# A fused cross attention and SwiGLU block: first weights made in the output weights' space, stores and spills as streams, six step orders re-dealt

## The chip, the cores and the metric

One core of one Trainium2 chip. The metric is the device time of one execution in microseconds; of several runs the median is taken. The engines have these names: PE is TensorE, PEld its weight loads, DVE VectorE, ACT ScalarE, POOL GpSimd, SP SyncE.

## The reference

```python
B, H, S, Ns, D = (8, 8, 512, 32, 64)
a = softmax(x @ state.T / sqrt(D));   xread = a @ state      # 512 tokens read 32 states
a2 = softmax(state @ x.T / sqrt(D));  sread = a2 @ x         # 32 states read 512 tokens
x = concatenate([xread, sread], axis=2)                      # heads side by side: (8 * 544, 512)
xn = x / sqrt(mean(x * x) + 1e-06) * rms_g
g = xn @ w_gate                                              # 512 x 1536
out = (silu(g) * (xn @ w_val)) @ w_out                       # 1536 x 512
```

So for each of 8 batches 512 token rows and 32 state rows are read by attention, scaled by RMS, and sent through three weight matrices. x and the states come as float32; the three weight matrices arrive in 64-bit form and are converted by the kernel itself.

## The kernel before

**The work of a batch.** For each batch the kernel loads the states (L137) and x (L142, L147, L155) and computes scores of all heads at once. For batches 2 and later x is transposed on DVE (L357, from `x_b` to `xB`), stored to memory as `x_d` from ACT's queue (L359), loaded back as `xG` by four DMAs from ACT's queue (L364), and multiplied with the states on PE (L374). The token read follows (L430 the exponential on ACT, L456 on PE, squares for the RMS at L463 on ACT, scaled rows `aT_s` at L469 on DVE). The state read goes the same way: exponentials on ACT (L629), a transpose on DVE (L647, `eB`), a store to `e_d` (L650) and four loads (L654) on ACT's queue, then the products with x on PE (L665). Since the rows of a token read are mixtures of only 32 states per head, gate and value weights are first multiplied with the states ("own weights": `own_weights`, PE L730, copied out by ACT at L742 as `v`, combined further by POOL).

**The feed-forward.** The 1536 columns are 12 blocks, taken as 6 pairs. Batch 0 goes plainly (`hidden`: PE L773, silu on ACT L779, product on DVE L783), its hidden rows `hb` are spilled to memory as `h_d` (L785) and projected at the very end. Batches 1 to 7 and the state rows use products in the manner of Strassen: `hidden_seven` makes seven products where eight would stand (PE L882; copies out on ACT L929, L932, L934; silu on ACT L936; sums on DVE L945, L958). The projection is `project_seven` for batch 1 and the states, `project_twice` (two levels, PE L1170, ACT L1183, POOL L1198, DVE L1210 to L1229) for the others. Its weights are sums of quarters of the output weights, kept in memory as `t_d`.

**The weights.** The raw weights arrive as 18 pieces of 1 MB, gate and value of each pair in turn and then six output pieces; four raw buffers let four pieces be under way, and the load of piece k+4 (L240) is issued when piece k has been converted (ACT L273 and L276, DVE L297 and L301). The tile `wo` (12 blocks of 512 columns) takes the output weights. Gate weights and value weights of a pair share one tile of 1 MB. In the kernel before, it lies in the pool `ws` of three buffers (`new_w`, name `w_m`), and when its value part is converted, SP stores it to memory as `w_d` (L305). From then on every batch fetches its six pairs from `w_d` into the three `ws` buffers again (L222), pair n+3 when pair n has been used.

**The order of the work.** Nothing is scheduled automatically on PE, DVE, ACT, POOL and SP: each stage is a generator ("stream") that issues a few instructions per step, and strings of letters say which stream takes the next step. ORDER covers batch 0 (letters that include the preparation), batch 1 (lower case) and batch 2 (upper case), PERIOD is used for each of batches 3 to 6, LAST for batch 7 and STATES for the state rows together with batch 0's projection. An engine works through its instructions strictly in the order issued, and a DMA is issued by the engine in whose program it stands: a waiting instruction holds up all behind it on that engine.

Of the kernel before, what the change touches and what calls it, by code (L numbers as in the profile page):

```python
# [21 lines left out]
W_BUFS = 3  # L22
# [1 line left out]
ZERO = 16 * 896  # L24

ORDER = (
    "zzzz11z11113111zzzz18883133121228221119991998825515222z1662262666116622665555511"
    "9226122880226666644200955555889988i446666655i99ji000iijmm888i5i6995998990jj66i80"
    "0iimm896988966669j000ijimii86899j8mm899000i68ii8906i9666666666jm800jm88i6998i6ij"
    "j7796767imm7ni877777jnnnn8nnnnihht799798mtv89ht7788hhuuthuuhh9thu9txhhhtuuxxfff8"  # L30
    "8hu99qqvqtvhahxtthhhtxuuhxhuuuhxaaxhtutthaahtfhxvxxqaaqfuhhuutuuhthhthtLaauhuhuu"
    "uthhutxhtaaqhhthhhquualuuuutuhuuaaaaaaaaqqaaaaaaaaaaauppppaqppaakkccckdaqquapaaa"
    "dkaaaaapaccawcwxxxssssspwxVssddsskpkkkppkkpdddddddddddddxfsXkxkssspsssddddddddHH"
    "dccddTHTHTHUXXUVVHHTTHTUHHTUUHHHHHUUUHTXTHTTlAXAAAXAHHHAHHUUUUTTXXUTAHHUUXFTVXXX"
    "HHHHHeUUUTUHTHUUUTHHKTHHGAHKKAUAAeUUTUHeKTHTHHUUUTUUHUTUUAAAAAHUUKAPPPPCPPKKFPKK"
    "KKPPPPKKKKCAPPPPKKPPPPAAAAAAAPPPCGPPKKKPPKPKPPCCCFFAAAAAAGGAAAKKKKKKAFSAPPPPPSSP"
    "SSAKAAPPPPAAAAASSSSSPPKPKOOPSSKOAOPAWWWXXXXXKGLPGKPKKKKOOXPSSCPPGFSSCOO"
)

PERIOD = (  # L40
    "vahhthtxthahhhhxuutxuthahaaathatuuhluhhuhtvtvfxutuxhaxhthaghuaxhhxuauutfuxhhukkk"
    "tthhhthgauvuhtuhhkthtauhaaxaxtauhhuausufufxhutsththhaugauuthuhuughupaptuhsuuupkg"
    "kpkkpkkapppkcppkkpkppcgpppkkpkaapopkspaaapkpkkpppasacpkaaccksppkpkkpcaakspkpaaak"
    "asaappskpksspskppkaakppkgoooppppkaakappppkasoalwfswossxpxfxcwxxxcoo"
)

LAST = (
    "fvhthhtthxxhuuthuxvvuhththuhhhthhuuthattxxxuahhhuutuhuhvhxxxtuththhhauuhtuuhkkff"
    "fhatxhuukhtthxxhuguhthhuuuutuuhhtahthhthuuuutuuupphupkkkpkkkupppkppkkkpppccppppp"
    "pppkkkkkkkkkkkkkkkkkaappppppppgcppppcpcggkpppaackkkkpppakkoooopppppppcpppkcoooo"  # L50
)
STATES = (
    "hthththhhyyyyyuutuuhththuhthrrrhhuutyrhthtyuhyyyhhtrhhuuuuuyhyytytrhthhthhhhhuuu"
    "uuhyyyyyytththhthhhuuuuuuuKKKthuuuuKKththhtuhuuKKtuPPughuKKKKPPPPPPPbguCgPPKPgKK"
    "KgKggPPKKCPPPPbPPPPKKKbKKKKKKKPPPPPPCCPPPPPKPKCPPPPOOCKbbKKKPKPPbKKKKKKOPKOOPPPP"
    "CPPPbCOppkpkkccppkkOOkcpkkpkpc"
)


# [1 line left out]
def kernel(  # L61
# [20 lines left out]
    nc = tc.nc  # L82
    VE, SE, GE, TE = nc.vector, nc.scalar, nc.gpsimd, nc.tensor

    B, H, S, D = x.shape
# [4 lines left out]
    NI = DM // P  # L90
    NM = DFF // P
# [102 lines left out]
    w_d = [scratch.tile([P, NI, 2, 2, P], F32, name="w_d%d" % mp) for mp in range(NM // 2)]  # L194
# [17 lines left out]
    raw = {}  # L212

    def new_w(n):

        w_sb[n] = ws.tile([P, NI, 2, 2, P], F32, name="w_m")
        return w_sb[n]

    def fetch(n):

        if NM // 2 <= n < (B + 1) * (NM // 2):
            nc.sync.dma_start(out=new_w(n), in_=w_d[n % (NM // 2)])  # L222
# [57 lines left out]
    def values():  # L280
        for k in range(len(pieces)):
            for a in parts(k):
                if a.start == 0:
                    to = home(k)
                    if k in raw:
                        words = raw[k].rearrange("p f four -> p (f four)").bitcast(U32)
                        words = words[:, 0:16 * P].rearrange("p (f two) -> p f two", two=2)[:, :, 1]
                dst = to[:, a]
                if k not in raw:
                    src = pieces[k].rearrange("p a (c f) -> p a c f", f=P)  # L290
                    for i in range(a.start, a.stop):
                        nc.sync.dma_start(out=to[:, i], in_=src[:, i])
                    yield
                else:
                    c = columns(k, a)
                    word, rest = words[:, c], words[:, c].bitcast(I32)
                    VE.tensor_scalar(rest, word, 2.0 ** -13, 2.0 ** 19 - 1, op0=ALU.mult, op1=ALU.min)  # L297
# [3 lines left out]
                    VE.tensor_tensor(out=dst.bitcast(I32), in0=rest, in1=top, op=ALU.bitwise_or)  # L301
                if a.stop == pieces[k].shape[1]:
                    mp, kind = places[k]
                    if kind == 1:
                        nc.sync.dma_start(out=w_d[mp], in_=w_sb[mp])  # L305
                    raw.pop(k, None)
                    load_piece(k + RAW_AHEAD)
                yield
# [453 lines left out]
    def hidden(m, lhs, rhs):  # L762


        gp, vp = [], []
        t = []
        h = hb[:, m, :]

        def products():
            for k, to in enumerate((gp, vp)):  # L770
                to.append((fx.tile([P, S], F32, name="f") if m % 2 else vps.tile([P, S], F32, name="pv")))
                for i, r in enumerate(rhs):
                    TE.matmul(out=to[0], lhsT=lhs(i, k), rhs=r,  # L773
                              start=(i == 0), stop=(i == len(rhs) - 1))
# [12 lines left out]

        return products(), silu(), gated()
# [583 lines left out]
    def first_batches():  # L1372
# [75 lines left out]
```

## Time and profile before

| | |
|---|---|
| median of 3 runs | 760.8 us (759.03 to 761.41) |
| profiled execution | 761.82 us |
| its span | 759.8 us |
| mean granted PE clock | 0.993 |
| PE busy | 739.1 us, 97% |
| DVE busy | 576.9 us, 76% |
| ACT busy | 355.4 us, 47% |
| POOL busy | 265.3 us, 35% |
| moved by DMA | 152.46 MB, mean 201 GB/s |

How to read it: the span runs from the first to the last recorded instruction, and some 2 us of the execution's time lie around it. The shares are means over very different stages: batch 0 with the conversion of the weights (to about 88 us), batch 1 (to about 137), batch 2 (to about 260), then periods of 80 us each for batches 3 to 7, and the state rows with batch 0's projection at the end.

### The profile page before, as it was taken

To read this page: it belongs to the slowest core of one execution; us is meant where nothing else is said; L and a number is where in the kernel's file an instruction comes from. 1 tells how busy PE (TensorE), PEld (TensorE's weight loads), DVE (VectorE), ACT (ScalarE), POOL (GpSimd) and SP (SyncE) were. 2 spreads that over 40 slices of the span, in tenths; PEclk is the share of its full clock that TensorE was granted. 3 is DMA by queue.
4 is the path that set the end of the run, shared out by engine and by line. 5 is a ranking of instruction groups with operands and counts; after the bars stand their busy time and mean duration, and the time that the engine had idled before them with its cause. 6 is when DMAs were issued, how large, how long until landed. Compare 5 with 4: busy or idle time off the path is not lost.

```text
span 759.8 us, 14397 instructions
## 1 busy us (share of the span) xinstructions
PE 739.1 (97%) x5660; PEld 605.3 (80%) x5660; DVE 576.9 (76%) x963; ACT 355.4 (47%) x616; POOL 265.3 (35%) x360
## 2 busy tenths in 40 slices
PE   8998989999999799999999999999999999999998
PEld 7532567777888677997799878987898689999997
DVE  5886678979699747994799469955998368977952
ACT  5987974433543255626472547335642552122110
POOL 1400534043402644129312851266223761330451
PEclk9999999999999999999999999999999999999999
DMA  8999896048636582378518870877166722256421
GB/s 233 361 364 418 298 408 195 6 141 300 265 79 268 167 319 56 134 266 276 159 56 300 261 217 1 302 238 261 29 256 201 268 105 63 77 209 228 126 63 53
DMA packets 60667, 152.46 MB, mean 201 GB/s; under 512 B 10420, under 2 KB 30392, under 8 KB 53688
## 3 DMA queue, kind: packets, MB, share of 16 engines
q1 hardware_dynamic: 49552, 132.59, 49.1%
q10 hardware_dynamic: 11048, 18.95, 8.7%
q8 instruction: 45, 0.74, 0.4%
q14 instruction: 22, 0.18, 0.1%
HBM read 119.61 MB, written 31.92 MB: 199 GB/s over the span
## 4 chain that ended last, share of the span: by engine, by line
PE 72%; DVE 11%; DMA 9%; ACT 4%; issue 3%; POOL 1%; SPq 0%; ACTq 0%; DVEq 0%; POOLq 0%
PE f L882 30%; PE f L1170 26%; PE f L1026 5%; DMA w_m<-w_d 4%; PE pv L730 3%; DMA x_d<-xB 2%; DMA raw<-in_moe_w_val_dram 2%; PE at L730 1%; PE pv L773 1%; DVE w L1124 1%; PE at L374 1%; PE f L1318 1%; ACT ex L276 1%; DVE hb L958 1%; ACT lin L273 1%
## 5 line engine op out<-in xcount | busy, mean ns | idle before, releaser
L882 PE MATMUL f<-aT_s,v 128*128 128x256 f32 x504 | 119.5, 381 | 0.7 <-ACT g L934 0.7
L882 PEld LDWEIGHTS f<-aT_s,v 128*128 128x128 f32 x504 | 94.6, 190 | 22.2 <-DVE h L1224 3.4
L945 DVE TENSOR_TENSOR g<-g,f 128x512 f32<-128x512 f32 x84 | 56.1, 685 | 62.8 <-PE f L882 41.6
L882 PE MATMUL f<-aT_t,vs 128*128 128x256 f32 x336 | 86.8, 382 | 2.0 <-ACT g L929 2.0
L1183 ACT COPY kept<-f 128x512 f32<-128x512 f32 (+1 forms) x56 | 29.9, 536 | 110.0 <-PE f L1170 110.0
L1198 POOL TENSOR_TENSOR kept<-kept 128x256 f32<-128x256 f32 x28 | 21.6, 771 | 167.2 <-DVE kept L1210 114.1
L1170 PE MATMUL f<-w,h 128*128 128x128 f32 x588 | 74.7, 276 | 0.2 <-DVE h L1220 0.2
L882 PEld LDWEIGHTS f<-aT_t,vs 128*128 128x128 f32 x336 | 62.7, 190 | 14.1 <-issue 4.4
L757 POOL TENSOR_TENSOR vs<-v 128x256 f32<-128x256 f32 x42 | 32.1, 764 | 116.7 <-ACT v L742 116.5
L1170 PEld LDWEIGHTS f<-w,h 128*128 128x128 f32 x588 | 69.8, 192 | 0.7 <-DVE h L1220 0.4
L936 ACT ACTIVATE hb<-g 128x1024 f32<-128x1024 f32 x42 | 44.4, 1057 | 49.5 <-DVE g L945 45.0
L318 POOL TENSOR_TENSOR ri<-ss,mhalf 128x4 f32<-128x4 f32 (+1 forms) x9 | 8.5, 948 | 116.7 <-ACT ss L406 103.2
L958 DVE TENSOR_TENSOR hb<-hb,f 128x512 f32<-128x512 f32 x42 | 28.6, 682 | 24.6 <-PE f L882 24.5
L882 PE MATMUL f<-aT_t,v 128*128 128x256 f32 x168 | 43.9, 383 | 0.0
L882 PE MATMUL f<-aT_s,vs 128*128 128x256 f32 x168 | 43.4, 380 | 0.0
L1170 PE MATMUL f<-wo,hb 128*128 128x128 f32 x336 | 42.3, 275 | 0.0
L1170 PE MATMUL f<-wo,h 128*128 128x128 f32 x336 | 42.1, 275 | 0.0
L1170 PEld LDWEIGHTS f<-wo,hb 128*128 128x128 f32 x336 | 40.3, 192 | 1.1 <-issue 0.8
L958 DVE TENSOR_TENSOR hb<-hb,c 128x512 f32<-128x512 f32 x42 | 32.9, 784 | 9.4 <-ACT hb L936 9.2
L1170 PEld LDWEIGHTS f<-wo,h 128*128 128x128 f32 x336 | 39.8, 192 | 0.0
L934 ACT COPY g<-f 128x512 f32<-128x512 f32 x42 | 24.8, 590 | 31.1 <-PE f L882 31.1
L882 PEld LDWEIGHTS f<-aT_t,v 128*128 128x128 f32 x168 | 31.0, 190 | 9.1 <-issue 3.4
(256 smaller groups left out, 1659.5 us busy)
## 6 DMA issues: line engine op xcount, KB each, us to landing
w_m<-w_d SPq DMA_DIRECT2D x48, 1024.0 KB, 7.2
w<-t_d SPq DMA_DIRECT2D x49, 576.0 KB, 6.7
out_dram<-kept SPq DMA_DIRECT2D x32, 256.0 KB, 4.1
raw<-in_moe_w_val_dram SPq DMA_DIRECT2D x6, 1024.0 KB, 9.7
w_d<-w_m SPq DMA_DIRECT2D x6, 1024.0 KB
raw<-in_moe_w_out_dram SPq DMA_DIRECT2D x6, 1024.0 KB, 12.4
x_b<-in_x_dram SPq DMA_DIRECT2D x6, 1024.0 KB
x_d<-xB ACTq DMA_DIRECT2D x6, 1024.0 KB, 5.5
```

Source lines behind the costliest of these rows:

```text
L318: GE.tensor_tensor(out=ri[:, 0:n], in0=ss, in1=mhalf[:, 0:n], op=ALU.pow)
L730: TE.matmul(out=pv[e][Ns * j:Ns * j + Ns, :], lhsT=stT_g[b][D * e:D * e + D, j, :], rhs=w[D * e:D * e + D, j].rearrange("p m k f -> p (m k ...
L757: GE.tensor_tensor(out=vs[:, 0], in0=a21, in1=a22, op=ALU.add)
L882: TE.matmul(out=ps[:, i, 0:half], lhsT=l[:, i, :], rhs=r, start=(start and i == 0 and k == 0), stop=(k == len(lhs) - 1), skip_group_check= ...
L934: SE.copy(gates(q)[1], q["x"][:, :, 0:half])
L936: SE.activation(out=hid(2 * mp, 2 * mp + 2)[:, :, 0:n].rearrange("p m (c t) -> p m c t", c=2), in_=q["g"][:, :, :, 0:half], func=ACTF.Silu ...
L945: VE.tensor_tensor(out=to, in0=to, in1=q[ps][:, :, 0:half], op=ALU.add)
L958: VE.tensor_tensor(out=part, in0=part, in1=val, op=ALU.mult)
L1026: TE.matmul(out=banks[name][:, r, :], lhsT=lhs(k)[:, P * r:P * r + P], rhs=rhs(k), start=(start and r == 0 and k == 0), stop=(k == HM - 1) ...
L1170: TE.matmul(out=to[half][:, slot, :], lhsT=lhs[:, k, :], rhs=rhs[:, k, :], start=(fresh and n in (0, 4) and k == 0), stop=(k == QM - 1), s ...
L1183: SE.copy(of_half(k, i), banks[name][i])
L1198: GE.tensor_tensor(out=k[:, 4:8:3], in0=k[:, 5:6].to_broadcast([P, 2, QD]), in1=k[:, 4:8:3], op=ALU.add)
```

## The change

1. The converted gate and value weights of pairs 0 to 2 are made in the `ws` buffers and stay there for batch 1, which no longer fetches them. Those of pairs 3 to 5 are made in `wo`, into whose space the output weights come later.
2. The six stores to `w_d` and the six spills to `h_d` are no longer issued by the steps that finish the values, but by two streams of their own, "b" and "y", whose place is given by letters.
3. All orders are dealt anew, with the same letters but for the 12 new ones: ORDER has 883 steps instead of 871; the counts of PERIOD, LAST and STATES are the same.

```diff
 def fetch(n):
-        if NM // 2 <= n < (B + 1) * (NM // 2):
+        if NM // 2 + W_BUFS <= n < (B + 1) * (NM // 2):
             nc.sync.dma_start(out=new_w(n), in_=w_d[n % (NM // 2)])
 def home(k):
...
-        return (w_sb[mp] if kind else new_w(mp))[:, :, :, kind, :]
+        if kind == 0:
+            first_w[mp] = (new_w(mp) if mp < W_BUFS else
+                           wo[:, NI * (mp - W_BUFS):NI * (mp - W_BUFS) + NI].rearrange(
+                               "p i (m k f) -> p i m k f", m=2, k=2))
+            w_sb[mp] = first_w[mp]
+            if mp < W_BUFS:
+                w_sb[mp + NM // 2] = first_w[mp]
+        return first_w[mp][:, :, :, kind, :]
 def values():
...
-                    mp, kind = places[k]
-                    if kind == 1:
-                        nc.sync.dma_start(out=w_d[mp], in_=w_sb[mp])
                     raw.pop(k, None)
                     load_piece(k + RAW_AHEAD)
 def gated():
             VE.tensor_tensor(out=h, in0=t[0], in1=vp[0], op=ALU.mult)
-            if m % 2:
-                nc.sync.dma_start(out=h_d[m // 2], in_=hb[:, m - 1:m + 1])
             yield
+    def weights_kept():
+        for mp in range(NM // 2):
+            nc.sync.dma_start(out=w_d[mp], in_=first_w[mp])
+            yield
+    def gated_kept():
+        for mp in range(NM // 2):
+            nc.sync.dma_start(out=h_d[mp], in_=hb[:, 2 * mp:2 * mp + 2])
+            yield
...
-                   "z": keep_awake()}
+                   "b": weights_kept(), "y": gated_kept(), "z": keep_awake()}
```

Of the four strings the beginning of PERIOD stands for all:

```diff
-    "vahhthtxthahhhhxuutxuthahaaathatuuhluhhuhtvtvfxutuxhaxhthaghuaxhhxuauutfuxhhukkk"
+    "vhhaththhaaatuhhhaauxxavvutthhtthhhhxuuuuututhhuhxxthtuaahuhhuaaxxtutfghlhukktht"
```

What the new strings do to the programs of the engines is seen in rows of those programs. In the changed kernel the line numbers are 5 to 30 higher. First SP in batch 0 and the beginning of batch 1, before: raw pieces (L240), stores of weights (`w_d`, L305), spills (`h_d`, L785), fetches (L222).

```order
L305 DMA w_d_129<-w_m 128x2048
L240 DMA raw<-in_moe_w_val_dram 128x4x1024
L785 DMA h_d_136<-hb 128x1024
L240 DMA raw<-in_moe_w_gate_dram 128x4x1024
L305 DMA w_d_130<-w_m 128x2048
L240 DMA raw<-in_moe_w_val_dram 128x4x1024
L240 DMA raw<-in_moe_w_gate_dram 128x4x1024
L785 DMA h_d_137<-hb 128x1024
L305 DMA w_d_131<-w_m 128x2048
L240 DMA raw<-in_moe_w_val_dram 128x4x1024
L240 DMA raw<-in_moe_w_out_dram 128x2x2048
L222 DMA w_m<-w_d_128 128x2048
```

The same stretch now (raw pieces L249, stores L1277, spills L1283, fetches L224, x L143):

```order
L1277 DMA w_d_129<-w_m 128x2048
L249 DMA raw<-in_moe_w_val_dram 128x4x1024
L249 DMA raw<-in_moe_w_gate_dram 128x4x1024
L249 DMA raw<-in_moe_w_val_dram 128x4x1024
L249 DMA raw<-in_moe_w_out_dram 128x2x2048
L1277 DMA w_d_130<-w_m 128x2048
L1277 DMA w_d_131<-wo 128x2048
L249 DMA raw<-in_moe_w_out_dram 128x2x2048 x3
L1277 DMA w_d_132<-wo 128x2048
L1277 DMA w_d_133<-wo 128x2048
L249 DMA raw<-in_moe_w_out_dram 128x2x2048 x2
L1283 DMA h_d_136<-hb 128x1024
```

The store of the third pair moved from among the gate and value pieces to behind the first output piece, the spills moved behind the last raw piece, and the first fetch of all is now that of `w_d_131`, after x of batch 2 has been issued.

Second, ACT around the store and the loads of x in batch 3, before (`g`, `hb` and `c` are the seven products' copies and silus, `v` the own weights):

```order
L359 DMA x_d_135<-xB 128x4x512
L934 COPY g<-f 128x2x256
L936 ACTIVATE hb<-g 128x1024
L929 COPY g<-f 128x2x256
L742 COPY v<-at 128x512
L932 COPY c_3156<-f 128x512
L742 COPY v<-at 128x512
L364 DMA xG<-x_d_135 32x4x512
L934 COPY g<-f 128x2x256
L364 DMA xG<-x_d_135 32x4x512 x2
```

And now (store L365, loads L370, the copies L933, L936 and L938, silu L940, own weights L748):

```order
L365 DMA x_d_135<-xB 128x4x512
L940 ACT_TABLE_LOAD
L940 ACTIVATE hb<-g 128x1024
L933 COPY g<-f 128x2x256
L936 COPY c_3111<-f 128x512
L938 COPY g<-f 128x2x256
L940 ACTIVATE hb<-g 128x1024
L933 COPY g<-f 128x2x256
L748 COPY v<-at 128x512 x2
L936 COPY c_3149<-f 128x512
L938 COPY g<-f 128x2x256
L370 DMA xG<-x_d_135 32x4x512 x4
```

Between the store and the first load 6 instructions stood, and now 11 stand, and the four loads go together.

Third, ACT at the turn from batch 2 to batch 3, before (exponentials L629, squares' sums L406, `e_d` stored at L650 and loaded at L654):

```order
L629 ACTIVATE e_2123,z_2126<-sS,s_2124 128x4x128 x2
L406 ACTIVATE ss<-at,bounds 32x4 x4
L650 DMA e_d_143<-eB 128x1024
L654 DMA e_2123<-e_d_143 32x4x256 x4
L742 COPY v<-pv 128x512 x2
```

And now (exponentials L635, `e_d` stored at L656, squares L469, kept parts of the projection L1187, `e_d` loaded at L660):

```order
L635 ACTIVATE e_2039,z_2042<-sS,s_2040 128x4x128
L656 DMA e_d_143<-eB 128x1024
L469 ACTIVATE sq<-pv 128x512
L1187 COPY kept<-f 128x384
L469 ACTIVATE sq<-pv 128x512
L469 ACTIVATE sq<-at 128x512 x2
L660 DMA e_2039<-e_d_143 32x4x256 x4
L412 ACTIVATE ss<-at,bounds 32x4 x4
L687 ACTIVATE sr<-at,z_2042 128x64 x2
L748 COPY v<-pv 128x512 x2
```

The store moved ahead of the squares and of their sums (L412), and five instructions now stand between it and the loads, which followed it directly before.

More of the change, by code (lines that the diff above doesn't have):

```diff
@@ L26 @@
 ORDER = (
[L27 to L37, printed above, removed]
+    "zzzz11z1133411441311zzz88z111111222229995288932665582255z66161816622552621299555"
@@ new lines @@
+    "88225551119900026115b255852226698ii908j6667668800ii99j7iii897mmb96776866666660ji"
+    "jmm00iii98998898866jm6900088ii997bb777jj98i66m000mi96886i998966ijbb666666ji08i80"
+    "46mi06688m99999iy8yy6jj886iijm778m7nnnnnninnnhthh9t8ytm88hhuuthhhttu99h99977vxxx"
+    "uhthhh8hhuuutttuhhth9qqqhvxxxvxxuufuuhhxahltaataatuuaahhhqutuhuhvhttuuhthhhtqqqq"
+    "xxxuaayuuuhuaahhttuhthhhyhthquuuuuuuqtaaaaaahuuuufppcaaacppcaacddaaaqppaaaaaaaak"
+    "kdddadkkaaakppaaaaafdcfcpdaassdsddaddssssssssapkLkkkwwxfwppxxddxkkfqppdddkscsddl"
@@ L38 @@
+    "dsdddddddcVxHHTTHTHHHHUUTTsAxHTAUUHUHHTHVVHXHAsAXXAAAUUUTTUHTHUHTXXXHUXXXHHHUTTH"
+    "TAUHHTAUUKeeAHHUUTAFVXHUUHTHTXXKKHHTKHHHAHHUUUUUUTTTeHHHHTHUAAAGAAAUUUUUUTGPPAAH"
+    "PPUUUCUPPPKKKKKKAAAPPKAPPKKCPPPPPPPPKPPPPKKKSKSFFAFSSKKPPPKKKAAPPCPPAAAAKPCCAPSS"
+    "KSPACAPKKPKKPPAGAASPPPOAAOPSSSAAAKAKAGPLSPPKOAOAPSSWWXXXWXXKKFFPCKPPKPKKOXGOSSCO"
+    "OGG"
 )
 PERIOD = (
-    "vahhthtxthahhhhxuutxuthahaaathatuuhluhhuhtvtvfxutuxhaxhthaghuaxhhxuauutfuxhhukkk"
-    "tthhhthgauvuhtuhhkthtauhaaxaxtauhhuausufufxhutsththhaugauuthuhuughupaptuhsuuupkg"
@@ L43 @@
-    "kpkkpkkapppkcppkkpkppcgpppkkpkaapopkspaaapkpkkpppasacpkaaccksppkpkkpcaakspkpaaak"
-    "asaappskpksspskppkaakppkgoooppppkaakappppkasoalwfswossxpxfxcwxxxcoo"
+    "vhhaththhaaatuhhhaauxxavvutthhtthhhhxuuuuututhhuhxxthtuaahuhhuaaxxtutfghlhukktht"
+    "xhkkuhuhuaavxhhtttaaxauuafxxhfuuhshthhhhuutuuahththhtsuuhuuutppuhaauuupauskkpppp"
+    "pcpkkpppppakpkkkkkgkfckakgaskkaakkppppppppapsappkoocccppcaaakkppasspaaakkapkksss"
+    "sppppppgppkpaakpgkppkooasalffaaapkkppcaakkkkaswwogosssgxxppxcoowxxx"
@@ L51 @@
 )
 STATES = (
[L53 to L56, printed above, removed]
+    "htyhhththhryyhhuuuyhtyuththhtuhhyuutuhhthyyyythhuuthhhuuuyyyyyyrrtththhhuutuuhhr"
+    "urrhhtuuyyuythtthuuyhhhuuhKtttKKKhhtuuuuhuhuthuPKuKPuhuKKKKKKKgPgPPPPPPPPPPPggCP"
+    "gggKPPKKKPCPPKPCCPPPKKKKKKPPKKKKKKKPKPPKPPCCPPPPPKKKKPPKPPPPKKKKPPPPPPOOOOOObbbP"
@@ L57 @@
+    "CbbbbCppkkkuccpppkkkkOcpkppkOc"
 )
@@ L212 @@
     raw = {}
+    first_w = {}
     def new_w(n):
```

6 lines of the change are left out of this document (3 added, 3 removed).

## The prediction

> **What bounds the kernel now.** I read the page's busy shares first, then a table of windows by stage, and then, engine by engine, the rows of the timeline that carry an idle time.
>
> ```profile
> span 759.8 us, 14397 instructions
> PE 739.1 (97%) x5660; PEld 605.3 (80%) x5660; DVE 576.9 (76%) x963; ACT 355.4 (47%) x616; POOL 265.3 (35%) x360
> ```
>
> TensorE (PE) is busy for 739.1 of 759.8 us, and the change issues the same matmuls. So whatever the change gives must come out of 20.7 us of idle PE, a few of them before the first matmul, and out of time in which PE ran at a lower clock. The windows say where both lie. Each row is a stretch in us, its length, busy time and count for PE, PEld, DVE, ACT, POOL, then the granted PE clock, the DMA share and GB/s.
>
> ```profile
> 29.30:64.00 34.70, 34.32 (x208) 12.91 (x207) 27.95 (x44) 30.07 (x37) 5.70 (x10) 1.00 0.99 365
> 64.00:68.00 4.00, 1.61 (x5) 0.40 (x3) 1.22 (x2) 2.96 (x4) 0.00 (x0) 1.00 1.02 429
> 68.00:71.60 3.60, 3.60 (x12) 1.07 (x20) 3.53 (x6) 3.00 (x5) 0.00 (x0) 0.53 1.01 416
> 71.60:88.40 16.80, 16.80 (x91) 7.56 (x92) 11.00 (x16) 14.95 (x25) 3.91 (x5) 1.00 0.80 298
> 88.40:137.00 48.60, 44.76 (x316) 33.62 (x315) 39.58 (x57) 29.06 (x42) 21.79 (x24) 1.00 0.81 289
> 260.00:263.30 3.30, 0.00 (x0) 0.00 (x0) 1.37 (x3) 0.00 (x0) 3.22 (x5) 0.92 0.84 287
> 263.30:270.00 6.70, 6.65 (x94) 4.78 (x95) 0.00 (x0) 1.64 (x5) 6.46 (x10) 0.53 0.84 292
> 430.40:510.40 80.00, 80.00 (x664) 68.41 (x663) 62.92 (x106) 40.15 (x74) 33.34 (x46) 1.00 0.60 199
> ```
>
> The last row is a steady batch: PE is never idle, DVE works 62.92 and ACT 40.15 of 80 us. Nothing can be won there, and something can be lost. The losses stand in four other places: batch 0 (up to 88.4), batch 1 (88.4 to 137), the end of batch 2 (260 to 270), and two later spots shown below.
>
> **Batch 0.** PE rows, then ACT, then the chain of waits:
>
> ```profile
> 67.98 3.61 PE L773 MATMUL pv<-aT_s,v 128*128 128x512 f32 x4 [2.39 <-ACT sq L463]
> 72.54 1.98 PE L773 MATMUL pv<-aT_s,v 128*128 128x512 f32 x4
> ```
> ```profile
> 65.01 1.25 ACT L273 ACTIVATE lin<-raw,bounds 128x1024 f32<-128x1024 int16 x1 [2.82 <-DMA raw<-in_moe_w_val_dram]
> ```
> ```profile
> 29.21 0.61 DVE raw L297
> 30.15 1.18 DVE w_m L301
> 50.15 0.34 SPq L305
> 50.59 14.34 DMA raw<-in_moe_w_val_dram
> ```
>
> PE waited 2.39 us for ACT's L463, which stood in ACT's program behind a conversion waiting 2.82 us for a raw weight piece. That piece took 14.34 us, and just ahead of it on SP, at 50.15, stands a 1 MB store of converted weights. At the 365 to 429 GB/s of these windows, 1 MB costs 2.4 to 2.9 us of the DMA engines, which are full (share 0.99 to 1.02): about the wait. Then the clock fell: the same four matmuls take 3.61 us instead of 1.98, and 3.60 us at 0.53 lose 3.60 x 0.47 = 1.7 us. So the place costs 4.1 us. In the new order the third store comes three pieces later and the spills of h come after the last raw piece, so both parts should go. Against it stands the start: the last write of aT_s on DVE now has a conversion of 1024 columns more ahead of it (0.61 + 1.18 = 1.8 us by the chain rows), so the first L773 comes about 2 us later. What is late next is ACT: its busy time from 29.3 to 88.4 is 30.07 + 2.96 + 3.00 + 14.95 = 51.0 us, and PE's need without the loss is 59.1 - 4.1 = 55.0 us. That is 4 us of slack. I take 4.1 - 2 = **+2.1**; bounds -1.9 (only the late start shows) and +4.1.
>
> [...]
>
> **Batch 1.** It no longer fetches the weights of pairs 0 to 2, since the first copies are kept.
>
> ```profile
> 91.83 1.09 PE L730 MATMUL pv<-w_m,stT_g 64*32 64x512 f32 x16 [0.45 <-DMA w_m<-w_d]
> 106.03 1.09 PE L730 MATMUL pv<-w_m,stT_g 64*32 64x512 f32 x16 [1.64 <-DMA w_m<-w_d]
> 130.71 1.10 PE L882 MATMUL f<-aT_t,vs 128*128 128x256 f32 x4 [1.35 <-ACT g L929]
> ```
> ```profile
> 89.52 16.46 DMA w_m<-w_d
> 119.06 8.76 DMA x_d<-xB
> ```
>
> The first two waits are for fetches, the second for one that took 16.46 us. Both fetches fall away: 0.45 + 1.64 = **+2.1**. Price of the cover: the next three pairs, made in the space of the output weights, are fetched into ws buffers that come free only when pairs 0 to 2 have been used. If that is late, the wait stands at pair 3 instead of pair 1 and nothing is gained: bounds 0 and 2.1. The output pieces must now wait for the stores that read their space. Their cost, from nothing to one conversion (0.61 + 1.18 us of DVE), lies inside batch 0's bounds.
>
> **Gathering x.** The 1.35 us at 130.71 is ACT's: the load of xG stands in ACT's program and waits for the store x_d, 8.76 us under way, and L936 and L929 queue behind it. The same happens once more later:
>
> ```profile
> 119.06 0.41 ACTq L359 DMA_DIRECT2D x_d<-xB  x1
> 127.84 0.82 ACTq L364 DMA_DIRECT2D xG<-x_d  x2
> 129.04 1.06 ACT L936 ACTIVATE hb<-g 128x1024 f32<-128x1024 f32 x1 [4.23 <-DVE wo L1009]
> ```
> ```profile
> 529.14 0.59 ACT L934 COPY g<-f 128x512 f32<-128x512 f32 x1 [2.88 <-PE f L882]
> ```
> ```profile
> 529.78 0.92 PE L882 MATMUL f<-aT_s,v 128*128 128x256 f32 x3 [0.72 <-ACT g L934]
> ```
> ```profile
> 518.92 9.85 DMA x_d<-xB
> ```
>
> Store to load is 8.8 us at the first place and 9.9 us at the second. Before, 4 ACT instructions stood between the two in batch 2 and 6 later; now 8 and 11. These come at PE's pace, so the distance about doubles, and neither wait should remain: 1.35 + 0.72 = **+2.1**, bounds 0 and 2.1. The score matmuls that need xG stay behind 54 matmuls of L882, as before, and three of four loads stand where they stood, behind the same copy. If that cover fails, it is at most the 4.23 us that ACT lost at 129.04.
>
> **The turn from batch 2 to 3.**
>
> ```profile
> 252.61 0.34 ACTq L650 DMA_DIRECT2D e_d<-eB  x1
> 255.31 1.76 ACTq L654 DMA_DIRECT2D e<-e_d  x4
> ```
> ```profile
> 263.35 1.93 PE L665 MATMUL at<-x_b,e 128*32 128x64 f32 x64 [3.39 <-issue]
> ```
>
> PE reaches L665 at 259.96 and waits 3.39 us. Its exponents go through memory: stored at 252.61, loaded from 255.31 on, so 10.7 us from store to first use. At the next steady turn the trace puts no idle time there, and the same matmuls take 1.03 us instead of 1.93. The clock row gives 6.70 us at 0.53, which lose 6.70 x 0.47 = 3.1 us: 6.5 us in all. In the new order the store stands 12 groups of L1170 ahead of L665; before it was 8 groups and two L730. Twelve groups of six at 0.67 us, by the chain of a steady turn,
>
> ```profile
> 425.29 1.03 PE at L665 x64
> 427.60 0.67 PE f L1170 x6
> 430.40 9.71 PE f L882 x44
> ```
>
> are 8.0 us. The trip needs 2.7 us to the store's landing (252.61 to 255.31), 1.76 for four issues, and the landing of the last load, which here ended at 263.35, 6.3 us after 257.07. A weight fetch was under way then, and the new order has none near. With the last part between nothing and 6.3 us the trip is 4.5 to 10.7 us, so the wait that is left lies between 0 and 2.7. I take 1.5 without a fall of the clock: 6.5 - 1.5 = **+5.0**, bounds 0 (a left wait of 2.4 us was enough to lower the clock in batch 0) and 6.5.
>
> **Own weights of pairs 3 and 4.** In each of five batches their products now come after 16 matmuls of L882 instead of 30; their fetches still start when pairs 0 and 1 have been used.
>
> ```profile
> 427.53 0.42 SPq L142 DMA_DIRECT2D x_b<-in_x_dram  x1
> 428.05 1.70 SPq L222 DMA_DIRECT2D w_m<-w_d  x2
> ```
> ```profile
> 598.87 1.21 PE L730 MATMUL pv<-w_m,stT_g 64*32 64x512 f32 x16 [1.14 <-DMA w_m<-w_d]
> ```
> ```profile
> 590.33 8.41 DMA w_m<-w_d
> ```
>
> L665 starts at 425.29 in this batch, the first L882 at 430.40, the two fetches at 428.05. A matmul of the program is two of the page's, so 16 of L882 take 32 x 9.71 / 44 = 7.1 us, and the product of pair 3 comes at about 437.5, 9.5 us after its fetch was issued. By the 8.41 us of the last row that is enough, by the 16.46 us of the fetch in batch 1 it is 7 us too little, once; two fetches go out together, and the product of pair 4 follows at once. I take a value near the first row, a wait of 0.4 us in each of five batches: **-2.0**; bounds 0 and -7.5 (1.5 us each, somewhat over the 1.14 of this place).
>
> **What costs nothing.** ACT_TABLE_LOADs fall from 24 to 16; in steady batches ACT has 40 us to spare (40.15 of 80). The wait of 1.14 us at 598.87 and the stage of the states I leave as they are, with bounds -2 and +1.1. The stores as streams of their own move the same bytes.
>
> [...]
>
> **Sum.** 2.1 + 2.1 + 2.1 + 5.0 - 2.0 = 9.3 us. The profiled execution took 761.82 us, its span 759.8 plus 2.0 around it; 761.8 - 9.3 = 752.5. It lies 1.0 above the median of the three runs, 760.8, so the forecast is **751.5 us**.
>
> **Rivals.** R1, a wait takes another's place: the fetches for pairs 3 and 4 land late in every batch. 1.5 us in five batches is 7.5 instead of 2.0, so 751.5 + 5.5 = 757.0. For it speaks the 1.14 us at 598.87, against it the steady batch without any idle PE.
>
> R2, slower: DVE's program now has two of the four transposes of x_b (L357) ahead of the first sum of the first pair (L945) and two right behind it; before, all four stood behind three such sums.
>
> ```profile
> 434.28 1.38 DVE L945 TENSOR_TENSOR g<-g,f 128x512 f32<-128x512 f32 x2 [7.73 <-PE f L882]
> 436.44 2.48 DVE L357 STREAM_TRANSPOSE xB<-x_b 128x512 f32<-128x512 f32 x4
> ```
>
> If x_b is not there, DVE stops and with it the sums that free PE's accumulators. Before, the transposes began at 436.44, 8.9 us after x_b was issued; the first sum starts at 434.28, 6.8 us after it. The new order issues x_b ahead of an output store, so somewhat sooner, and I put the point from which the mechanism decides at 9 us under way for x_b. At 12 us, between the 8.41 and 16.46 us of the two fetches of 1 MB above, DVE is blocked for 3 us; with 2.5 of it on PE in five batches that is 12.5 us: 751.5 + 12.5 = 764.0. Against it: DVE idles 17 us of a steady batch, and the fetch of 8.41 us is inside the 9.
>
> R3, the change doesn't give what it removes: batch 0 becomes ACT-bound (0 of 2.1) and the turn keeps its wait (0 of 5.0): 751.5 + 7.1 = 758.6, about no change.
>
> **How the numbers follow.** A measurement of this kernel can tell about 0.3%, or 2.3 us, from no change. Forecast (747 to 756) 0.57, R1 0.13, R2 0.18, R3 0.12. Of R3 two thirds fall within 0.3%, of R2 nearly all are slower, and the forecast and R1 are faster but for a small part of each: faster 0.68, same 0.14, slower 0.18. The range takes in the forecast's bounds below (all terms at their best and no loss at the fetches: 761.8 - 2.1 - 4.1 - 2.1 - 6.5 - 1.1 - 1.0 = 744.9, so 745) and reaches up to R2's 764, part of R2 left out above.
>
> **What would show it.** Right: no idle PE and no clock near 0.53 around 68 and 263 us; no fetch in batch 1 before pair 3; the loads of xG issued without ACT idle behind them. R1 would show as L730 released by the fetch about 12 us after each L665; R2 as DVE idle before L357, released by x_b, and PE idle at L882; R3 as PE waiting for ACT in batch 0. I am wrong if the new order makes waits at places where the old one has none, since I priced only the edits I could find in it.

## The result, and the profile after

The changed kernel takes 750.39 us at the median of four runs, the kernel before 760.04 us. The ratio is **0.9866, 95% interval 0.9837 to 0.9896**: 1.3% faster, about 9.7 us, where 751.5 us had been forecast. One run of the four, the profiled one, took 1930.91 us, PE busy for 1922.7 us of it with the same 5660 matmuls (the 504 of L886 from `aT_s` and `v` for 315.1 us instead of 120.2), so the profile read here is that of a second set of runs of the same kernel (750.22 us, ratio 0.9885, interval 0.9856 to 0.9914), whose profiled execution has this span and these busy times:

```profile
span 747.6 us, 14397 instructions
PE 733.0 (98%) x5660; PEld 604.5 (81%) x5660; DVE 576.7 (77%) x963; ACT 344.4 (46%) x608; POOL 262.3 (35%) x360
```

The span is 12.2 us shorter than that of before, more than the 9 to 10 us between the medians: the profiled execution of before was one of the slower ones of its kernel. The windows of the same stages, columns as before the prediction (length, the five engines' busy time, PE clock, DMA share, GB/s):

```profile
64.00:68.00 4.00, 4.00 (x24) 1.63 (x9) 2.97 (x3) 3.97 (x6) 0.00 (x0) 1.00 1.01 428
68.00:71.60 3.60, 3.60 (x23) 1.08 (x22) 3.38 (x7) 3.57 (x6) 0.00 (x0) 1.00 1.00 380
71.60:85.40 13.80, 13.80 (x127) 6.37 (x126) 10.43 (x16) 12.53 (x19) 5.51 (x7) 1.00 1.02 410
85.40:134.00 48.60, 48.60 (x281) 38.04 (x279) 43.32 (x66) 26.72 (x41) 17.43 (x23) 1.00 0.64 229
...
168.90:174.10 5.20, 0.08 (x1) 0.00 (x0) 3.34 (x6) 0.37 (x1) 0.87 (x1) 1.00 0.94 358
174.10:181.00 6.90, 6.86 (x95) 4.56 (x96) 1.67 (x4) 2.69 (x7) 2.82 (x4) 0.75 0.41 119
...
252.10:259.00 6.90, 6.90 (x139) 4.52 (x137) 5.26 (x7) 3.71 (x9) 6.59 (x9) 1.00 0.65 191
259.00:339.00 80.00, 79.81 (x662) 68.51 (x662) 63.77 (x106) 36.40 (x69) 34.84 (x48) 1.00 0.58 201
```

The places that were to be mended are mended: around 68 us PE is busy throughout at clock 1.00, batch 1 (85.4 to 134) has no idle PE, and the turn from batch 2 to 3 (now around 252) has neither idle time nor a low clock. A steady batch still has almost no idle PE (79.81 of 80 us). But the fifth row shows a hole that the kernel before did not have: 5.2 us without PE, then 6.9 us at a mean clock of 0.75. On PE these rows of the timeline stand at the turn from batch 1 to 2 and at the turn from batch 2 to 3:

```profile
174.15 1.93 PE L671 MATMUL at<-x_b,e 128*32 128x64 f32 x64 [5.17 <-DMA e<-e_d]
...
252.16 1.10 PE L671 MATMUL at<-x_b,e 128*32 128x64 f32 x64
```

L671 is the old L665, the state read. It waits 5.17 us at the turn from batch 1 to 2, where the kernel before waited for nothing. This wait is the only one of 0.4 us or more that is left on PE behind the start of batch 0.

Where the 12.2 us came from, by the first L882 of batch 1 and the following matmuls: batch 0 ends 3.0 us sooner (85.35 instead of 88.37), though its first L773 stands at 31.69 instead of 29.35. The waits of batch 1 that are gone sum to 0.45 + 0.41 + 1.64 + 1.35 = 3.9 us. The turn to batch 3 gave 3.39 us of waiting and 3.1 of low clock, three later waits 0.72 + 1.14 + 0.91 = 2.8 us. The new hole took 5.2 + 6.9 x 0.25 = 6.9 us back. These make 9.3; the rest lies in what these windows and gaps below 0.4 us do not single out. Measured from one batch's first L882 (now L886) to the next one's, the 12.2 us divide otherwise: 3.0 in batch 0, -0.1 in batch 1, 8.1 in batch 2, -1.5 in batches 3 to 6, 1.9 in batch 7 and 0.8 from there to the end. The two orders don't put the same work between these marks, and no wait of PE says why the four steady batches together became longer (322.4 us instead of 320.9).

### The profile page after: what moved, and what is told of

Same layout as the page of the kernel before. It is cut to its first block, busy times and chain, and to the rows that moved or that the text cites. A ratio compares the mean times of both kernels' runs of the same rounds, so it can differ in the third digit from the quotient of the medians.

```text
span 1929.1 us, 14397 instructions
## 1 busy us (share of the span) xinstructions
PE 1922.7 (100%) x5660; PEld 1340.1 (69%) x5660; DVE 578.6 (30%) x963; ACT 350.6 (18%) x608; POOL 254.6 (13%) x360
## 4 chain that ended last, share of the span: by engine, by line
PE 100%; ACT 0%; DVE 0%; issue 0%; ACTq 0%
PE f L886 42%; PE f L1174 32%; PE f L1030 8%; PE pv L736 3%; PE f L779 3%; PE pv L779 3%; PE at L736 2%; PE at L671 1%; PE at L462 1%; PE at L380 1%; PE f L1334 1%; PE at L331 0%; PE pv L541 0%; PE at L353 0%; PE at L534 0%; PE at L645 0%
## 5 line engine op out<-in xcount | busy, mean ns | idle before, releaser
L886 PE MATMUL f<-aT_s,v 128*128 128x256 f32 x504 | 315.1, 832 | 0.0
L886 PEld LDWEIGHTS f<-aT_s,v 128*128 128x128 f32 x504 | 175.6, 352 | 149.5 <-issue 131.1
L886 PE MATMUL f<-aT_t,vs 128*128 128x256 f32 x336 | 221.3, 833 | 0.0
L1174 PE MATMUL f<-w,h 128*128 128x128 f32 x588 | 188.2, 536 | 0.0
L1174 PEld LDWEIGHTS f<-w,h 128*128 128x128 f32 x588 | 181.2, 450 | 4.7 <-issue 4.6
L886 PEld LDWEIGHTS f<-aT_t,vs 128*128 128x128 f32 x336 | 121.8, 364 | 78.0 <-issue 77.5
L886 PE MATMUL f<-aT_s,vs 128*128 128x256 f32 x168 | 111.1, 828 | 0.0
L886 PE MATMUL f<-aT_t,v 128*128 128x256 f32 x168 | 110.9, 840 | 0.0
L1187 ACT COPY kept<-f 128x512 f32<-128x512 f32 (+1 forms) x56 | 29.8, 533 | 402.6 <-PE f L1174 390.0
L886 PEld LDWEIGHTS f<-aT_t,v 128*128 128x128 f32 x168 | 60.2, 368 | 45.6 <-issue 44.5
L1174 PEld LDWEIGHTS f<-w,hb 128*128 128x128 f32 x252 | 80.0, 437 | 11.6 <-issue 11.5
L886 PEld LDWEIGHTS f<-aT_s,vs 128*128 128x128 f32 x168 | 59.7, 356 | 38.5 <-issue 38.5
L1174 PE MATMUL f<-w,hb 128*128 128x128 f32 x252 | 85.9, 541 | 0.0
L1174 PE MATMUL f<-wt,h 128*128 128x128 f32 x252 | 80.8, 537 | 0.0
```

What stands on the lines that cost most here:

```text
L886: TE.matmul(out=ps[:, i, 0:half], lhsT=l[:, i, :], rhs=r, start=(start and i == 0 and k == 0), stop=(k == len(lhs) - 1), skip_group_check= ...
L1174: TE.matmul(out=to[half][:, slot, :], lhsT=lhs[:, k, :], rhs=rhs[:, k, :], start=(fresh and n in (0, 4) and k == 0), stop=(k == QM - 1), s ...
L1187: SE.copy(of_half(k, i), banks[name][i])
```

## The experiments

They are told in the order of the reasoning. Times are medians; each ratio is to the kernel before on the same chip.

**The changed kernel once more**, without an edit, is the run read above.

> The changed kernel once more, since the profile shown with the result has every matmul at less than half of its usual speed. By the prediction 751.5 us at the median, with no idle time and no clock near 0.53 around 68 us and at the turn from batch 2 to 3, and waits for weight fetches of 0.4 us in each of five batches. By rival R1 these waits are 1.5 us each; by R2 DVE waits for x_b; by R3 ACT holds up PE in batch 0.

Measured 750.22 us. None of the five waits for weight fetches came, so R1 does not hold. What became of R2 is seen on DVE, then on PE, in a steady batch:

```profile
340.75 1.30 DVE L363 STREAM_TRANSPOSE xB<-x_b 128x512 f32<-128x512 f32 x2 [5.32 <-DMA x_b<-in_x_dram]
```
```profile
346.93 1.09 PE L736 MATMUL at<-w_m,stT_g 64*32 64x512 f32 x16
```
```profile
335.27 0.38 SPq L143 DMA_DIRECT2D x_b<-in_x_dram  x1
336.33 2.98 SPq L224 DMA_DIRECT2D w_m<-w_d  x2
```

DVE does stand 5.32 us and is released by x_b, as R2 said, but x_b is there 5.5 us after its issue, and PE, with products of the first pair still to make, never stops. The own weights of pair 3 come at 346.93, 10.6 us after their fetch was issued, and wait for nothing.

**First pairs fetched again for batch 1.**

```diff
-        if NM // 2 + W_BUFS <= n < (B + 1) * (NM // 2):
+        if NM // 2 <= n < (B + 1) * (NM // 2):
...
-            if mp < W_BUFS:
-                w_sb[mp + NM // 2] = first_w[mp]
```

> The changed kernel, but batch 1 fetches the weights of pairs 0 to 2 again as the kernel before does (3 MB more), in the new order. If keeping the first copies is what took away the waits of 0.45 and 1.64 us in batch 1, they come back: 2.1 us slower than the changed kernel, about 752.5 us. Rival: the new order gives those fetches room enough and the kept copies are worth nothing in time: the same as the changed kernel, about 750.4 us.

Measured 751.99 us, ratio 0.9906 (0.988 to 0.9932): 1.8 us slower than the changed kernel by the medians. That is the size expected, but the two intervals overlap, so the size itself is not shown; and the waits do not stand at the place expected. No matmul waits for a fetched weight. PE has two waits that the changed kernel has not: for ACT at the end of batch 0 and at the start of batch 1, and ACT waits for raw pieces. First PE, then ACT:

```profile
80.46 1.99 PE L777 MATMUL f<-aT_s,v 128*128 128x512 f32 x4 [2.14 <-ACT t L783]
93.73 1.99 PE L884 MATMUL f<-aT_s,v 128*128 128x256 f32 x8 [2.01 <-ACT g L936]
```
```profile
78.54 1.25 ACT L280 ACTIVATE lin<-raw,bounds 128x1024 f32<-128x1024 int16 x1 [2.32 <-DMA raw<-in_moe_w_out_dram]
92.02 1.20 ACT L280 ACTIVATE lin<-raw,bounds 128x1024 f32<-128x1024 int16 x1 [2.40 <-DMA raw<-in_moe_w_out_dram]
```

So the fetches cost through the raw pieces under way beside them: ACT's waits of 2.32 and 2.40 us. The DMA engines were full already without them, at a share of 1.00 to 1.02 from 64 to 85.4 us in the changed kernel. The kernel before has the same neighbours on SP, where the prediction had looked only at the store ahead of the late piece (issued at 50.59):

```profile
54.55 0.87 SPq L222 DMA_DIRECT2D w_m<-w_d  x1
```

The first fetch for batch 1 was issued at 54.55, while the piece that landed at 65 was under way. That it delayed this piece is not shown by itself.

**Stores and spills at their old places.**

```diff
                 if a.stop == pieces[k].shape[1]:
+                    mp, kind = places[k]
+                    if kind == 1:
+                        nc.sync.dma_start(out=w_d[mp], in_=first_w[mp])
...
             VE.tensor_tensor(out=h, in0=t[0], in1=vp[0], op=ALU.mult)
+            if m % 2:
+                nc.sync.dma_start(out=h_d[m // 2], in_=hb[:, m - 1:m + 1])
```

The twelve letters "b" and "y" are taken out of ORDER with it.

> The changed kernel with the stores of weights and the spills of hidden rows issued at their old places, by the steps that finish the values; all else in the new order. If the stores held up the raw pieces in batch 0, the wait of 2.4 us and the low clock (1.7 us) come back at least in part: 2 to 4 us slower than the changed kernel, 752.5 to 754.5 us. Rival: batch 0 is bound by ACT in the new order, or by the sum of the bytes, and the place of the stores does not matter: 750.4 us.

Measured 750.26 us, ratio 0.9882 (0.9852 to 0.9912): the rival's number. With the fetches gone, the place of the stores costs nothing: from 31.7 to 64 us the DMA engines had a share of 0.85 in the changed kernel, and in this stretch SP issues four stores (33.03 to 59.99) and three spills (40.95 to 61.91) here instead of three stores, so they fill time that was free.

**Both together.** The two edits above in one kernel.

> The changed kernel with the first pairs fetched again for batch 1 and with the stores and spills at their old places, so only the new order, and the weights of pairs 3 to 5 made in the output weights' space, are left. Fetching back alone cost 1.8 us and the old places of the stores nothing. If the DMA engines are full in batch 0 and it is the bytes that count, the two add up: about 752 us. Rival: each was covered by the other, and together they bring back the whole wait of batch 0, 754 to 757 us.

Measured 755.98 us, ratio 0.9955 (0.9933 to 0.9978). They do not add up to 1.8 us; together they cost 5.8 by the medians, and this interval lies clear of that of the changed kernel. PE shows one wait in batch 0, larger than that of the kernel before:

```profile
83.80 3.68 PE L779 MATMUL f<-aT_s,v 128*128 128x512 f32 x4 [5.17 <-ACT t L785]
```

The matmuls behind it also run at about half speed (3.68 us instead of 1.98). In the changed kernel the DMA engines are full from 64 to 85 us (share 1.00 to 1.02 in the rows above). The stores at their old places alone leave no wait in batch 0, the fetches alone one of 2.14 us, both together one of 5.17. That the raw pieces have some slack in the new order, and that the two edits use up the same slack, fits this but was not measured by itself. So each of the two parts of the change is worth little beside the other (1.8 us and nothing), and about 4 to 6 us without it. What then is left of the change, the new order and the weights made in the output weights' space, still gives 0.9955 of the kernel before.

**The exponentials sent earlier, in the kernel before.** The steps of the transpose and the store at the turn from batch 2 to 3 move ahead of thirteen others:

```diff
-    "... SSPSSAKAAPPPPAAAAASSSSSPPKPK ..."
+    "... SSPSSSSAKAAPPPPAAAAASSSPPKPK ..."
```

> The kernel before with one move: at the turn from batch 2 to 3 the transpose of the exponentials and their store to memory stand ahead of the squares' sums, about 1.4 us earlier. If the trip through memory sets the start of the state read, the wait of 3.39 us falls to about 2.0 and, if the clock then keeps up, 3.1 us more go: 755.5 to 758.6 us. Rival: the loads are late for the weight fetch that runs beside them, and the wait stays: 760 us.

Measured 759.79 us, ratio 0.9997 (0.9975 to 1.0019): no gain. Yet the wait at L665 is gone. It stands earlier, first on PE, then the reason on DVE:

```profile
252.32 0.58 PE L401 MATMUL at<-part,groups 128*128 128x16 f32 x2 [3.23 <-DVE part L398]
...
263.67 1.10 PE L665 MATMUL at<-x_b,e 128*32 128x64 f32 x64
```
```profile
247.09 1.25 DVE L647 STREAM_TRANSPOSE eB<-e 128x1024 f32<-128x1024 f32 x1 [1.64 <-ACT e L629]
...
251.49 0.69 DVE L398 TENSOR_REDUCE part<-sq 128x16 f32<-128x512 f32 x1
```

The transpose of 1.25 us, and the 1.64 us that DVE waits for its input, now stand ahead of the squares, and PE waits 3.23 us for their sum. The window behind it ran at clock 0.50:

```profile
252.30:258.00 5.70, 5.68 (x27) 5.70 (x28) 1.63 (x5) 1.02 (x4) 3.59 (x5) 0.50 0.35 92
```

So at this turn two ways lead to the state read, one through DVE's squares and one through memory, and moving DVE time from one to the other moved the wait.

**The exponentials sent later, in the changed kernel**, the reverse move:

```diff
-    "... PSSKSPACAPKKPKKPPAGAASPPPO ..."
+    "... PSKPACAPKKPKKPPAGAASSSPPPO ..."
```

> The changed kernel with one move at the turn from batch 2 to 3: the transpose of the exponentials and their store stand directly ahead of the loads, as in the kernel before, so behind the squares. If the length of the trip from the store to the state read sets that turn, the store comes about 3.5 us later and a wait of about 3 us with a low clock is back: 3 to 6 us slower than the changed kernel, 753 to 756 us. Rival: the wait went because DVE has less behind it there, and the place of the store does not matter: 750 us.

Measured 752.37 us, ratio 0.9907 (0.9875 to 0.994), between the two numbers; its interval and that of the changed kernel overlap for the most part. The wait at L671 does not come back. ACT's queue and ACT, then PE:

```profile
248.07 0.34 ACTq L656 DMA_DIRECT2D e_d<-eB  x1
250.78 1.76 ACTq L660 DMA_DIRECT2D e<-e_d  x4
252.59 1.06 ACT L412 ACTIVATE ss<-at,bounds 32x4 f32<-32x4 f32 x4 [5.49 <-DVE z L664]
```
```profile
254.80 0.65 PE L331 MATMUL at<-ident,ri 128*128 128x128 f32 x4 [1.13 <-POOL ri L324]
256.05 1.10 PE L671 MATMUL at<-x_b,e 128*32 128x64 f32 x64
```

A smaller wait stands ahead of it: 1.13 us for POOL's `ri`, which needs ACT's sums (L412), and these start only when ACT has issued the loads, at 252.5. From store to use it is 8.0 us, this wait included, and at L671 that is enough: the loads, done issuing at 252.5, are there at most 3.5 us later. In the kernel before 10.7 us were not enough. One thing that differs is the fetch beside the loads, which stood there in the kernel before and stands there in neither of these two runs of the new order, so that was tried next, at both turns.

**The fetches of batch 2's pairs 3 and 4 behind the state read, in the changed kernel**, two letters moved:

```diff
-    "... wwxfwppxxddxkkfqppdddkscsddld ..."
+    "... wwxwppxxddxkkqppdddkscsffddld ..."
```

> The changed kernel with two steps moved: the weight fetches of batch 2's pairs 3 and 4 are issued behind the state read of batch 2 instead of ahead of it. The changed kernel waits 5.17 us there for the exponentials' way through memory, 18.5 us long, at a DMA share near 1.0. If the transfers beside it make it that long, 2 MB less at about 0.4 MB per us take some 5 us off the trip, the wait falls to 0 to 1 us and the low clock behind it goes too: 5 to 8 us faster than the changed kernel, 742 to 745 us, if pairs 3 and 4 are not waited for afterwards. Rival: the trip is long for other reasons (its place on ACT, the loads' own small pieces): the wait stays, 750 us. A second rival: the wait moves to the weights of pairs 3 and 4, 748 to 752 us.

Measured **742.25 us, ratio 0.9782 (0.9749 to 0.9816)**: 8.0 us faster than the changed kernel by the medians (the ratios, each taken on its own chip, differ by 1.0%, 7.8 us) and 2.2% faster than the kernel before, the best of all. Here are ACT's queue of the changed kernel at that turn and SP's two fetches; PE's row stands with the result:

```profile
155.68 0.34 ACTq L656 DMA_DIRECT2D e_d<-eB  x1
162.75 1.93 ACTq L660 DMA_DIRECT2D e<-e_d  x4
```
```profile
157.69 0.32 SPq L224 DMA_DIRECT2D w_m<-w_d  x1
...
163.20 0.42 SPq L224 DMA_DIRECT2D w_m<-w_d  x1
```

And of the kernel with the late fetches:

```profile
161.19 1.82 ACTq L660 DMA_DIRECT2D e<-e_d  x4
```
```profile
168.39 1.10 PE L671 MATMUL at<-x_b,e 128*32 128x64 f32 x64
```

From the loads' issue to the state read it was 11.4 us (162.75 to 174.15), and it is at most 7.2 us (161.19 to 168.39) without a wait. No wait has moved to pairs 3 and 4. The wait itself is no chance of one execution: in the four other profiles whose order is the same at this turn, those of the fetches back, the old stores, both together and the late exponentials, it is 4.64 to 5.82 us.

**One of the two fetches.** In the first kernel (the first line with +) only the second fetch moves; in the other (the last line) the first takes the second's place and the second moves.

```diff
-    "... wwxfwppxxddxkkfqppdddkscsddld ..."
+    "... wwxfwppxxddxkkqppdddkscsfddld ..."
+    "... wwxwppxxddxkkfqppdddkscsfddld ..."
```

> The changed kernel with only one of the two fetches moved behind the state read of batch 2: the first is still issued ahead of the exponentials' loads, beside their store, the second (issued at 163.20, beside the loads) is not. If every MB in the queues lengthens the trip alike, half of the 8 us go: about 746 us, with a wait of 2 to 3 us. Rival: only what stands beside the loads counts: 742 us.

> The changed kernel with one fetch at the place of the second, beside the exponentials' loads, and the other behind the state read of batch 2, so that nothing is fetched beside the exponentials' store. If every MB lengthens the trip alike: about 746 us, as with the other half. Rival: only what stands beside the store counts, 742 us; or only what stands beside the loads, 750 us.

Measured 742.82 us (ratio 0.9792, 0.9758 to 0.9827) with a fetch left beside the store, 748.02 us (0.9856, 0.9821 to 0.9891) with a fetch left beside the loads. Of the first kernel, SP's fetch, ACT's loads and PE:

```profile
157.33 0.32 SPq L224 DMA_DIRECT2D w_m<-w_d  x1
```
```profile
161.37 2.79 ACTq L660 DMA_DIRECT2D e<-e_d  x4
```
```profile
168.55 1.10 PE L671 MATMUL at<-x_b,e 128*32 128x64 f32 x64
```

In the other the wait is still there:

```profile
162.00 0.42 SPq L224 DMA_DIRECT2D w_m<-w_d  x1
```
```profile
161.74 1.85 ACTq L660 DMA_DIRECT2D e<-e_d  x4
```
```profile
171.67 1.10 PE L671 MATMUL at<-x_b,e 128*32 128x64 f32 x64 [3.18 <-DMA e<-e_d]
```

So not every MB counts alike: the fetch issued 0.26 us after the first of the loads makes them late (9.9 us to the state read), and one issued 4.0 us ahead of them does no harm here (at most 7.2 us). The store lands no later for it either: from store to loads it is 6.0 us with that fetch beside the store and without it.

**The fetch of before's turn from 2 to 3 behind the state read, in the kernel before.**

```diff
-    "... KKKAFSAPPPPP ... KKKKOOXPSSCPPGFSSCOO"
+    "... KKKASAPPPPP ... KKKKOOXPSFSCPPGFSSCOO"
```

> The kernel before with one step moved: at the turn from batch 2 to 3 the weight fetch that SP issued at 256.96, beside the loads of the exponentials, is issued behind the state read. If that fetch makes the loads late, the wait at L665 (3.39 us in the profile of before, 0.84 in the profile of the kernel with the moved loads of x, which has the same order here) goes to 0 to 0.5 us, and the low clock after it too: 2 to 5 us faster than the kernel before, 754 to 757 us. Rival: DVE's backlog there sets the end, or other transfers take the fetch's place: the time stays at 759 us.

Measured 755.88 us against 760.19, ratio 0.9966 (0.9939 to 0.9992): faster, but by the ratio 2.6 us, with an interval from 0.6 to 4.6. SP of the kernel before, then ACT's queue and PE of this run:

```profile
256.96 0.32 SPq L222 DMA_DIRECT2D w_m<-w_d  x1
```
```profile
254.99 1.76 ACTq L654 DMA_DIRECT2D e<-e_d  x4
```
```profile
259.76 1.10 PE L665 MATMUL at<-x_b,e 128*32 128x64 f32 x64
```

Loads issued as late as before (254.99, before 255.31) are now used 4.8 us later instead of 8.0, without a wait. The fetch had been issued 1.65 us after the first of them. The profile of before names no releaser for its wait ("issue"), so this run is what ties the wait to the loads: the same cause as at the other turn, tried in the other kernel. The gain is smaller, though, and a part of it is lost further on, where PE waits for ACT's L934, the copy next to the loads of x in ACT's program, and the profile of before has no wait:

```profile
284.39 1.99 PE L882 MATMUL f<-aT_s,v 128*128 128x256 f32 x8 [1.94 <-ACT g L934]
```

The run with the exponentials sent earlier has 1.37 us there, so it is not the moved fetch alone that makes it.

**The loads of x later, in the kernel before.** The first two of the four load steps stand with the last two, in ORDER and PERIOD:

```diff
-    "... htLaauhuhuuuthhutxhtaaqhh ..."
+    "... htLuhuhuuuthhutxhtaaaaqhh ..."
```

> The kernel before with one move: the first two of the four loads of x (batch 1 and batches 3 to 6) stand with the other two, some ACT instructions later. If ACT's wait for the landing of x's store is what stops PE at 130.71 and 529.78, these two waits go: 1.35 + 0.72 = 2.1 us faster than the kernel before, about 757 us. Rival: the scores then wait for xG instead, and the time stays at 759 us.

Measured 758.68 us, ratio 1.0001 (0.9979 to 1.0024): the rival's number. ACT no longer holds up PE at the first of the two places, but the scores wait for xG, 0.42 + 1.24 = 1.66 us where 1.35 had been. At the second place the 0.72 us are gone, and 0.38 us for another of ACT's copies stand there.

```profile
130.05 1.01 PE L374 MATMUL at<-xG,stT 64*32 64x512 f32 x2 [0.42 <-DMA xG<-x_d]
132.31 1.09 PE L374 MATMUL at<-xG,stT 64*32 64x512 f32 x14 [1.24 <-DMA xG<-x_d]
...
258.89 1.10 PE L665 MATMUL at<-x_b,e 128*32 128x64 f32 x64 [0.84 <-issue]
264.61 1.13 PE L882 MATMUL f<-aT_s,v 128*128 128x256 f32 x4 [1.70 <-ACT kept L1183]
```

The last two rows are from the same profile, at the turn from batch 2 to 3, where this kernel's order is that of before: 0.84 us instead of 3.39, and no matmul there at half speed, but 1.70 us for ACT's L1183 behind it, which the profile of before has not. The fetch stands beside the loads in both (1.65 and 1.67 us after the first). Why the loads took 5.5 us to the state read here and 8.0 there stays open. The place that the prediction priced at 6.5 us costs between 2.5 (0.84 + 1.70) and 6.5 us in one and the same order.

## Why the prediction was right, and where not

**Batch 0, +2.1 forecast.** The first L773 came 2.3 us later (31.69 instead of 29.35, 2 forecast), the wait and the low clock are gone, and batch 0 ends 3.0 us sooner. The late start cost less than the 2 us set down for it, since PE filled a part of it with other work: up to 31.7 us it had worked 27.66 us, before 28.91, so it was 1.25 us behind. ACT did not become the bound (R3). The size was about right, but the cause was put too narrowly: the stores ahead of the late piece were named, and at their old places they cost nothing alone. The fetches alone bring back 2.14 us of waiting in batch 0, and with the old places of the stores it is 5.17 us.

**Batch 1's fetches, +2.1.** The waits of 0.45 and 1.64 us are gone. With the fetches back in the new order the medians differ by 1.8 us, near the forecast, but they come by another way: no matmul waits for a fetched weight there, and PE waits for ACT and ACT for raw pieces. The step that does not hold is where the fetches are paid for.

**Gathering x, +2.1.** Both waits are gone in the changed kernel, 1.35 + 0.72. The reason given was that the distance from store to loads about doubles. It did not: from 8.8 us it became 8.1 at the first place and from 9.9 it became 11.3 at the second (before, ACT's wait for the store is a part of it). At the first place the 8.76 us that the store took before would still have been too long, so it must have landed sooner. In the kernel before, later loads alone moved the first wait to the scores. What else the new order does for xG was not tried by itself. The rows that bear on the first place are SP's and ACT's; of the kernel before

```profile
104.02 15.23 SPq L222 DMA_DIRECT2D w_m<-w_d  x4
```

and of the changed kernel

```profile
104.57 0.32 SPq L224 DMA_DIRECT2D w_m<-w_d  x1
```
```profile
109.17 0.41 ACTq L365 DMA_DIRECT2D x_d<-xB  x1
117.23 0.82 ACTq L370 DMA_DIRECT2D xG<-x_d  x2
```

Before, four fetches were issued from 104.02 to 119.25, the last of them at the time of x's store (119.06); now the last is issued 4.6 us ahead of the store. That would fit the cause found at the two turns, but it is argued and not shown. At the second place it does not hold: there the changed kernel, too, has a fetch beside x's store (SP issues the fetch at 506.35, ACT the store at 506.72 and the loads from 518.02 on), and no wait follows. The 11.3 us from store to loads are more than the 9.85 that the store took before, as the prediction meant it.

**The turn from batch 2 to 3, +5.0.** The wait and the low clock went, 6.5 us in the profiled execution. The trip through memory did decide, and the fetch beside it made it long (8.0 us from the loads to the state read, 4.8 with the fetch moved), as the working noted in passing. The place of the store, twelve groups ahead, on which the 1.5 us of a wait that is left rested, mattered less: with the store some 3 us later the trip of 8.0 us is enough at L671, and 1.13 us are lost ahead of it. And the 6.5 us were the price of one unlucky execution: the other profile of that order has 0.84 and 1.70.

**Own weights, -2.0.** Nothing was lost at these products: those of pair 3 come 10.6 us after their fetch and wait for none. The steady batches did become longer, by 1.5 us over four of them, for a reason that no row here shows.

**What was missing** is the turn from batch 1 to 2. The prediction named as a sign of its being wrong that the new order makes waits at places where the old one has none, since it had priced only the edits that it could find; this is such a place. It looked at e_d's trip where it was short of time, and did not ask of the other turns what now stands on SP beside the loads. There the new order issues a fetch 0.45 us behind the first of them, and with that fetch issued later the kernel is 7.4 us faster (742.82 instead of 750.22). It was offset by smaller terms: the own weights' 2.0 that did not come, the 1.5 and 0.9 by which the turn to batch 3 and batch 0 gave more than forecast, and 1.14 + 0.91 us of later waits that were costed at nothing. These make 6.5 us. So that 751.5 came so near to 750.4 is in good part luck: a loss of 7 to 8 us that was not in the sum, and gains that were not in it either. The mechanism of the forecast, waits of PE removed by a new order and by fewer transfers in batch 0 and 1, was right.

The streams by themselves give nothing that the runs show: with the stores at their old places, issued without the streams, the kernel takes 750.26 us against 750.22. And in the wait that was missed ACT's loads and SP's fetch are issued by different engines, and still the fetch delays the loads, 9.9 us to the state read against at most 7.2.

## What to carry to other kernels

How long a small round trip through memory takes can hang on one large transfer issued beside it: here 9.9 us from loads to use with a 1 MB fetch 0.26 us behind the first load, at most 7.2 without. When an order is dealt anew, go through every place that has such a trip, not only those that waited before, and list what other engines' queues issue within a microsecond or two of its loads; issuing one 1 MB fetch 4.2 us later, or 4.7 us earlier, was worth 7.4 and 5.2 us here. Two savings in the same stretch need not add, and here they did not (taken back alone 1.8 us and nothing, together 5.8): take each back alone and both together before saying what one is worth. And before pricing a wait from one profile, look for the same place in a second execution of the same order.

## What the runs showed of the hardware

The fall of the clock is not set by the length of the wait alone. A wait of 2.39 us in batch 0 of the kernel before was followed by 3.6 us at clock 0.53; in the run with the moved fetch of before's turn, behind one of 2.19 us at the same place four matmuls took 3.08 us instead of 1.98. In the run with the exponentials sent earlier, whose batch 0 is the same, nearly the same wait had no such cost: four matmuls took 1.98 us at once, and the clock was 1.00 from 68.1 to 71.7 us.

```profile
68.13 1.98 PE L773 MATMUL pv<-aT_s,v 128*128 128x512 f32 x4 [2.36 <-ACT sq L463]
```

So one wait of 2.4 us is followed by the low clock and another is not; what decides it is not shown by these runs. The 1.7 us of the prediction's first term were therefore a matter of the execution.
